# Instruction blocks of 256 in a kernel's planner, and the first group's joins written out chunk by chunk

## The chip, the cores and the metric

The kernel runs on one core of a Trainium2 chip. The metric is the device time of one execution in microseconds, the median of several runs. Engines: TensorE (PE, with its weight loads PEld), VectorE (DVE), ScalarE (ACT), GpSimd (POOL), and SyncE (SP), which issues the DMAs.

## The reference

A delta-rule attention runs over 768 tokens for 4 x 8 heads of width 48, and its output goes through a gated product with weights of 384 x 1536, 384 x 1536 and 1536 x 384.

```python
k_n = k / (np.linalg.norm(k, axis=-1, keepdims=True) + 1e-06)
state = np.zeros((B, H, D, D)); y = np.zeros_like(q)
for t in range(S):
    kt, vt, bt = k_n[:, :, t], v[:, :, t], beta[:, :, t, None]
    y[:, :, t] = einsum('bhd,bhde->bhe', q[:, :, t], state)
    v_old = einsum('bhde,bhd->bhe', state, kt)
    state = state + bt[..., None] * einsum('bhd,bhe->bhde', kt, vt - v_old)
x = y.transpose(0, 2, 1, 3).reshape(B * S, H * D)
out = ((x @ w_a) * (x @ w_b)) @ w_out
```

## The kernel before, in words

The 768 tokens are cut into 24 chunks of 32, the chunks into 6 groups of 4. All 32 heads are worked on together: 4 heads stand side by side on the 128 partitions, 8 times along the free axis, so that each step is a group of 32 small matmuls on a quarter of the array (each shows as 64 matmuls and 64 weight loads, since a float32 matmul is two).

For each group the program has three streams. `prep(g)` loads k, v and the transposed k and q, and makes the products of keys with keys and queries (matmuls `bank<-rawb`, or `late` for some chunks). `solve(g)` inverts the triangular matrices of the 4 chunks together on VectorE (lines 785 to 794, tiles `b` and `tmp`). In groups 0 and 1 (`HALVES`) only the two 16-wide diagonal halves are inverted so, and the rest is joined by matmuls, chunk by chunk: a product (`bank<-b,tt`, `wp`), a copy of it scaled by -1 on ScalarE (`wr`), a matmul that copies the halves into a bank (`bank<-b,mk`, `xp`), a product added to it (`bank<-wr,xn`), and a copy to `tt` on ScalarE. `steps(g)` carries the state through the chunks: for each chunk a copy `sh` of the state, products with it (`bank<-sh,rawb`), `f` on VectorE, the product with `tt` (`bank<-f,tt`; in chunk 0 `bank<-vnb,tt`), a copy `u`, the state's update (`S_ps<-u,knb`), the product `bank<-u,at`, and then y, its transpose, and the two float16 halves of x (`xb`). Two chunks make one block of 256 tokens of x.

The streams `w0` to `w11` decode one block of 128 columns of the three weights each and split it into two parts; for the first four (`LOWS`) the lower part is made with two matmuls (`bank<-wh,zi` and `bank<-wh,neg` and the like). `moe(s, fcs)` multiplies block s of x with weight blocks: two groups of nine matmuls (`bank<-xb,wh`), then the gate on ScalarE and VectorE (`a`, `g`, `ghl`), then in `moe_out` two groups of three matmuls (`bank<-wo,ghl`) that add up in banks kept over all the weight blocks of the call. `QUEUE` says which blocks of x meet which weight blocks first.

Nothing is issued in the order in which it is written. `Plan.add` collects the operations with an estimated duration; `Plan.link` finds what depends on what, from the order in which they were written and the memory that they touch; `Plan.order` then makes an order for each engine and all of them are issued so (line 449 issues every operation, line 440 the fillers). The order comes from `pack`, a list scheduler that goes through the time and gives each engine the ready operation of the lowest priority number: at first the place in the program less `URGENCY` and `BOOST` of its stream (group 0's streams and the product's other engines have the largest). A backward pass then gives new priorities, and it is done six times (`PASSES`); the order with the shortest planned total is kept. `pack` also gives out the PSUM banks: six in the pool, of which one is kept back until 60 us of planned time (`UNTIL`) for fillers, matmuls on a tile of ones that are issued wherever the planner sees TensorE idle after 1.5 us (`IDLE`, `SINCE`), so that its clock stays up.

For TensorE `pack` counts instructions as `words` (4 for a float32 matmul, 2 for another). Before, a store of 512 words (`STORE`) was filled again at 0.070 words per ns (`FETCH`), and an operation with more words than were in store was put off:

```python
words, seen = min(self.STORE, words + (t - seen) * self.FETCH), t
if words < ops[i].words:
    heapq.heappush(wait[e], (t + (ops[i].words - words) / self.FETCH + 1.0, i))
```

The order in which the streams are written down is at lines 1042 to 1051: all of `prep` and `solve` of group 0, weight blocks 0 and 1, all of group 0's `steps`, weight blocks 2 to 5; `merge` then takes product and group 1's streams in turns.

Of the kernel before, what the change touches and what calls it, by code (L numbers as in the profile page):

```python
# [28 lines left out]
GROUPS = [list(range(i, i + 4)) for i in range(0, NCH, 4)]  # L29
# [3 lines left out]
HALVES = [1, 1, 0, 0, 0, 0]  # L33
# [27 lines left out]
class Plan:  # L61
# [203 lines left out]
    def pack(self, pri, back=False):  # L265

        ops, n = self.ops, len(self.ops)
        nxt = self.pred if back else self.succ
        left = [len(x) for x in (self.succ if back else self.pred)]
        engs = sorted({o.eng for o in ops})  # L270
        wait = {e: [] for e in engs}
        can = {e: [] for e in engs}
        free = {e: 0.0 for e in engs}
        ready, at, stop, done, dma = [0.0] * n, [0.0] * n, [0.0] * n, [], 0.0
        until, use, warm = self.WINDOW, 0.0, back
        words, seen = self.STORE, 0.0
        kept = 0 if back else 1
        vacant, held, blocked = [(k, {}) for k in range(len(self.pool) - kept)], {}, []
        fill = {}
        for i, o in enumerate(ops):  # L280
            if not left[i]:
                heapq.heappush(wait[o.eng], (0.0, i))
        while len(done) < n:
            best = None
            for e in engs:
                if can[e]:
                    t = free[e]
                elif wait[e]:
                    t = max(free[e], wait[e][0][0])
                else:  # L290
                    continue
                if best is None or t < best[0]:
                    best = (t, e)
            if best is None:
                raise RuntimeError("no order found")
            t, e = best
            if kept and t >= self.UNTIL:
                kept = 0
                vacant.append((len(self.pool) - 1, {"PE": t}))
                for k in blocked:  # L300
                    heapq.heappush(wait[ops[k].eng], (t, k))
                blocked = []
            while wait[e] and wait[e][0][0] <= t:
                i = heapq.heappop(wait[e])[1]
                heapq.heappush(can[e], (pri[i], i))
            i = None
            while can[e] and i is None:
                i = heapq.heappop(can[e])[1]
                if ops[i].words and not back:
                    words, seen = min(self.STORE, words + (t - seen) * self.FETCH), t  # L310
                    if words < ops[i].words:
                        heapq.heappush(wait[e], (t + (ops[i].words - words) / self.FETCH + 1.0, i))
                        i = None
                        continue
                need = [] if back else [b for b in ops[i].banks if b not in held]
                if need:
                    at_ = sorted((self.clear(ends, i), k) for k, ends in vacant)
                    if len(at_) < len(need):
                        blocked.append(i)
                        i = None  # L320
                    elif at_[len(need) - 1][0] > t:
                        heapq.heappush(wait[e], (at_[len(need) - 1][0], i))
                        i = None
                    else:
                        for b, (_, k) in zip(need, at_):
                            held[b] = [k, self.users[b], {}]
                        vacant = [x for x in vacant if x[0] not in {k for _, k in at_[: len(need)]}]
            if i is None:
                continue
            o = ops[i]  # L330
            if not back and not o.banks and self.HOLD:

                soon = t + min(self.HOLD, 0.8 * o.dur)
                nxt_ = [r for r, k in wait[e] if t < r < soon and pri[k] < pri[i] - self.MARGIN]
                if nxt_:
                    heapq.heappush(can[e], (pri[i], i))
                    for x in can[e]:
                        heapq.heappush(wait[e], (min(nxt_), x[1]))
                    can[e] = []
                    continue  # L340
            at[i] = t
            words -= o.words
            if e == "PE" and not back:

                if kept:
                    f, took, many = max(free[e], self.SINCE), self.IDLE * (1 if warm else 2), 0
                    while f + took <= t:
                        while until <= f:
                            warm = use > 0.43 * self.WINDOW if warm else use > 0.75 * self.WINDOW
                            use, until = 0.0, until + self.WINDOW  # L350
                        took = self.IDLE * (1 if warm else 2)
                        use, f, many = use + took, f + took, many + 1
                    fill[i] = many
                    words = max(0.0, words - 4 * many)
                while until <= t:
                    warm = use > 0.43 * self.WINDOW if warm else use > 0.75 * self.WINDOW
                    use, until = 0.0, until + self.WINDOW
                took = o.dur if warm else o.cold
                full = took * o.use / o.dur
                part = min(1.0, (until - t) / took)  # L360
                use += full * part
                if part < 1.0:
                    warm = use > 0.43 * self.WINDOW if warm else use > 0.75 * self.WINDOW
                    use, until = full * (1 - part), until + self.WINDOW
            else:
                took = o.dur
            free[e] = end = stop[i] = t + took
            for b in () if back else o.banks:
                h = held[b]
                h[1] -= 1  # L370
                h[2][e] = max(h[2].get(e, 0.0), end)
                if not h[1]:
                    vacant.append((h[0], h[2]))
                    for k in blocked:
                        heapq.heappush(wait[ops[k].eng], (t, k))
                    blocked = []
            if e == "SP":
                if back:
                    end = t + o.dur + self.MOVE[0] + o.move + self.MOVE[1]
                else:  # L380
                    dma = max(dma, t + o.dur + self.MOVE[0]) + o.move
                    end = dma + self.MOVE[1]
            done.append(i)
            for k, late in nxt[i]:
                ready[k] = max(ready[k], end + late)
                left[k] -= 1
                if not left[k]:
                    heapq.heappush(wait[ops[k].eng], (ready[k], k))
        return at, stop, done, max(stop), ({b: h[0] for b, h in held.items()}, fill)

    MOVE = (900.0, 1100.0)
    FETCH = 0.070
    IDLE, SINCE, UNTIL = 440.0, 1500.0, 60e3
    STORE = 512.0
    SWITCH = 180.0
    HOLD = 300.0
    MARGIN = 5000.0
# [3 lines left out]
    def order(self):  # L401
# [3 lines left out]
        ops = self.ops  # L405
# [11 lines left out]
                self.pred[i].append((j, late))  # L417
        pri, best = [o.pri - boost(o) - 1e12 * (o.stream == 'load') for o in ops], None
        for _ in range(self.PASSES):
            at, stop, done, total, bind = self.pack(pri)  # L420
            if best is None or total < best[0]:
                best = (total, at, stop, done, bind)
            _, stop, _, total, _ = self.pack([-t for t in stop], True)
            pri = [k - 1e12 if o.stream == 'load' else total - t - boost(o) for k, (o, t) in enumerate(zip(ops, stop))]
# [28 lines left out]
def tile_kernel(ctx, tc, kqt, kn, vn, beta, w, masks, out):  # L453
    nc = tc.nc
    plan = Plan(nc)
# [311 lines left out]
    def solve(g):  # L767
# [35 lines left out]
        for ci, c in enumerate(chs):  # L803
            tts[c] = ttr()
            if HALVES[g]:
                wp = att()[:, 0:128].rearrange("p (q t) -> p q t", t=16)
                with plan.group():
                    for q, h4, _, _ in heads():
# [5 lines left out]
                            stop=True,  # L814
                            skip_group_check=True,
                        )
                wb_ = wr()
                A.activation(wb_, wp, AF.Copy, scale=-1.0)
                xp = att()[:, 0:256].rearrange("p (q t) -> p q t", t=32)
                T.matmul(xp, eye, xtv[:, ci], start=True, stop=True, skip_group_check=True)  # L820
                with plan.group():
                    for q, h4, _, _ in heads():
# [5 lines left out]
                            stop=True,  # L828
                            skip_group_check=True,
                        )  # L830
                A.copy(tts[c], xp)
            else:
                A.copy(tts[c], xtv[:, ci])
        yield

    def steps(g):

# [120 lines left out]
    ops = {}  # L958
# [38 lines left out]
    def run_all(gen):  # L997
        for _ in gen:
            pass
# [41 lines left out]
    V.tensor_scalar_mul(negr, eye, -1.0)  # L1041
    run_all(pr[0])
    next(ws[0])
    run_all(sv[0])
    run_all(ws[0])
    run_all(ws[1])
    run_all(st[0])
    queue.extend(QUEUE)
    run_all(ws[2])
    run_all(ws[3])  # L1050
# [91 lines left out]
```

## Time and profile before

| | |
|---|---|
| median of 3 runs | 665.3 us (662.72, 665.30, 665.31) |
| profiled execution | 666.49 us, its span 664.4 us |
| mean granted TensorE clock | 0.982 |
| TensorE busy | 633.4 us, 95% of the span |
| VectorE, ScalarE busy | 404.2 us (61%), 272.9 us (41%) |
| DMA of data | 41.08 MB |

In the rows of the profile an instruction's tiles stand as output<-inputs, by the names above, with its line (L449 or L440), its engine and how many are merged; "[1.64 <-issue]" is idle time of the engine before it and what ended it, and "issue" means that nothing that the profile shows was waited for. Clock is the share of full speed that TensorE was granted.

### The profile page before, as it was taken

To read this page: it belongs to the slowest core of one execution; us is meant where nothing else is said; L and a number is where in the kernel's file an instruction comes from. 1 tells how busy PE (TensorE), PEld (TensorE's weight loads), DVE (VectorE), ACT (ScalarE), POOL (GpSimd) and SP (SyncE) were. 2 spreads that over 40 slices of the span, in tenths; PEclk is the share of its full clock that TensorE was granted. 3 is DMA by queue.
4 is the path that set the end of the run, shared out by engine and by line. 5 is a ranking of instruction groups with operands and counts; after the bars stand their busy time and mean duration, and the time that the engine had idled before them with its cause. 6 is when DMAs were issued, how large, how long until landed. Compare 5 with 4: busy or idle time off the path is not lost.

```text
span 664.4 us, 26616 instructions
## 1 busy us (share of the span) xinstructions
PE 633.4 (95%) x12238; PEld 539.0 (81%) x12238; DVE 404.2 (61%) x1059; ACT 272.9 (41%) x599; POOL 21.5 (3%) x33
## 2 busy tenths in 40 slices
PE   9988899889999999899999899999999999999997
PEld 7756688678888888788888688877888887888886
DVE  6956699659757896447964438953537863322222
ACT  3345683355535634324543326253322253332322
POOL 0100000000001200000200002000000000000000
PEclk9969999979999999999999999999999999999999
DMA  6847200501482000033000410000000000000000
GB/s 234 304 167 256 75 3 2 200 20 34 166 297 75 2 25 3 4 139 111 2 25 5 161 65 26 1 26 4 4 2 26 1 26 5 2 25 1 25 1 24
DMA packets 19983, 42.77 MB, mean 64 GB/s; under 512 B 1184, under 2 KB 4512, under 8 KB 19872
## 3 DMA queue, kind: packets, MB, share of 16 engines
q1 hardware_dynamic: 19872, 41.08, 17.7%
q8 instruction: 95, 1.56, 1.0%
q14 instruction: 16, 0.13, 0.1%
HBM read 36.36 MB, written 4.72 MB: 62 GB/s over the span
## 4 chain that ended last, share of the span: by engine, by line
PE 80%; DVE 12%; issue 4%; ACT 3%; ACTq 0%
PE bank L449 74%; DVE b L449 4%; PE S_ps L449 3%; DVE tmp L449 3%; PE bank L440 3%; DVE ghl L449 1%; ACT tt L449 1%; DVE g L449 1%; ACT ghl L449 1%; ACT a L449 0%; DVE vnb L449 0%; ACT u L449 0%; DVE wh L449 0%; DVE sc L449 0%; ACT sqf L449 0%
## 5 line engine op out<-in xcount | busy, mean ns | idle before, releaser
L449 PEld LDWEIGHTS <-wh 128*128 128x128 f16 x2592 | 242.7, 99 | 48.0 <-issue 16.3
L449 PE MATMUL bank<-xb,wh 128*128 128x256 f16 x2160 | 259.5, 274 | 0.8 <-DVE wh L449 0.8
L449 PE MATMUL bank<-wo,ghl 128*128 128x384 f32 x864 | 189.9, 354 | 0.2 <-DVE ghl L449 0.2
L449 PEld LDWEIGHTS bank<-wo,ghl 128*128 128x128 f32 x864 | 144.2, 189 | 4.2 <-issue 0.9
L449 ACT COPY a<-bank 128x256 f32<-128x256 f32 x144 | 53.6, 372 | 199.9 <-PE bank L449 199.6
L449 DVE TENSOR_TENSOR g<-bank,a 128x256 f32<-128x256 f32 x144 | 60.8, 422 | 102.4 <-ACT a L449 101.2
L449 ACT CAST ghl<-g 128x256 fp32r<-128x256 f32 x144 | 58.1, 403 | 68.3 <-DVE g L449 67.8
L449 DVE TENSOR_TENSOR ghl<-g,ghl 128x256 fp32r<-128x256 f32 x144 | 61.3, 426 | 34.3 <-ACT ghl L449 32.4
L449 PE MATMUL bank<-late,wh 128*128 128x256 f16 x432 | 54.1, 278 | 0.0
L449 DVE TENSOR_TENSOR tmp<-b,b 128x31 f32<-128x31 f32 (+20 forms) x154 | 51.2, 332 | 2.9
L449 DVE TENSOR_TENSOR b<-b,tmp 128x31 f32<-128x31 f32 (+20 forms) x154 | 50.6, 328 | 2.7
L449 DVE SCALAR_TENSOR_TENSOR y<-bank,sc,y 128x384 f32<-128x384 f32 x23 | 14.2, 617 | 55.0 <-ACT y L449 55.0
L440 PE MATMUL bank<-ones 128*128 128x256 f32 x106 | 29.0, 430 | 1.0 <-DVE ones L449 1.0
L449 ACT COPY sh<-S_ps 112x768 f32<-112x768 f32 x23 | 18.4, 798 | 27.5 <-PE S_ps L449 27.3
L449 PEld LDWEIGHTS bank<-sh,rawb 48*64 48x64 f32 x1216 | 20.6, 134 | 11.1 <-issue 8.9
L449 PE MATMUL bank<-sh,rawb 48*64 48x48 f32 x1216 | 23.8, 221 | 5.3 <-issue 5.2
L449 PE MATMUL bank<-u,at 32*32 32x48 f32 x1536 | 23.4, 203 | 4.8 <-issue 4.8
L449 DVE TENSOR_TENSOR f<-vnb,bank 128x384 f32<-128x384 f32 x38 | 20.2, 545 | 10.5 <-PE bank L449 10.5
L449 PEld LDWEIGHTS bank<-u,at 32*32 32x32 f32 x1536 | 19.0, 105 | 8.7 <-issue 7.5
L440 PEld LDWEIGHTS bank<-ones 128*128 128x128 f32 x106 | 22.1, 215 | 4.5 <-DVE ones L449 1.0
L449 PEld LDWEIGHTS S_ps<-u,knb 32*48 32x48 f32 x1216 | 16.2, 123 | 10.6 <-ACT u L449 4.3
L449 PEld LDWEIGHTS bank<-f,tt 32*32 32x32 f32 x1472 | 17.6, 106 | 8.8 <-issue 4.1
(115 smaller groups left out, 550.6 us busy)
## 6 DMA issues: line engine op xcount, KB each, us to landing
late<-in_w SPq DMA_DIRECT2D x10, 1152.0 KB, 6.0
rawb<-in_kqt SPq DMA_DIRECT2D x10, 1024.0 KB, 7.7
out<-late SPq DMA_DIRECT2D x24, 192.0 KB, 1.9
knb<-in_kn SPq DMA_DIRECT2D x10, 384.0 KB, 4.2
vnb<-in_vn SPq DMA_DIRECT2D x10, 384.0 KB, 4.9
wh<-in_w SPq DMA_DIRECT2D x2, 1152.0 KB, 6.3
late<-in_kqt SPq DMA_DIRECT2D x2, 1024.0 KB, 5.7
late<-in_kn SPq DMA_DIRECT2D x2, 384.0 KB, 3.9
```

The source lines that it names most:

```text
L440: self.nc.tensor.matmul(self.pool[-1][:, 0:256], self.idle, self.idle.unsqueeze(1).broadcast_to([P, 2, P]), start=True, stop=True, skip_gr ...
L449: fn(*(self.place(a, lease) for a in args), **{k: self.place(a, lease) for k, a in kw.items()})
```

## The change

It has two parts. In `pack`, the store of words is replaced by blocks of 256 instructions: `pos` counts the instructions given out, `come` the times at which blocks are there. Two blocks are there at the start; when the first instruction of a block is given out, the next begins to load, and is there 3.5 us later, or 5.0 us if the planner's own DMA traffic is still under way. An operation that would reach a block before it is there is put off by the difference. The fillers count as well. A pass that finds no order now ends the search instead of the program.

In the program, group 0's joins are written out one chunk at a time, each followed by the three steps of its chunk; weight blocks 0 and 1 come behind all of them. In each join the matmul that copies the halves (`xp`) is given an extra dependency on the scaled copy (`wr`). In group 1 each join is a portion of its own in the turns with the product, four portions where there was one.

```diff
@@ -273,7 +273,7 @@
         free = {e: 0.0 for e in engs}
         ready, at, stop, done, dma = [0.0] * n, [0.0] * n, [0.0] * n, [], 0.0
         until, use, warm = self.WINDOW, 0.0, back
-        words, seen = self.STORE, 0.0
+        pos, come = 0, [0.0, 0.0]
         kept = 0 if back else 1
         vacant, held, blocked = [(k, {}) for k in range(len(self.pool) - kept)], {}, []
         fill = {}
@@ -292,7 +292,7 @@
                 if best is None or t < best[0]:
                     best = (t, e)
             if best is None:
-                raise RuntimeError("no order found")
+                return None
             t, e = best
             if kept and t >= self.UNTIL:
                 kept = 0
@@ -307,9 +307,9 @@
             while can[e] and i is None:
                 i = heapq.heappop(can[e])[1]
                 if ops[i].words and not back:
-                    words, seen = min(self.STORE, words + (t - seen) * self.FETCH), t
-                    if words < ops[i].words:
-                        heapq.heappush(wait[e], (t + (ops[i].words - words) / self.FETCH + 1.0, i))
+                    slip = self.fetch(t, ops[i].words, ops[i].dur if warm else ops[i].cold, pos, come, dma)[0]
+                    if slip > 1.0:
+                        heapq.heappush(wait[e], (t + slip, i))
                         i = None
                         continue
                 need = [] if back else [b for b in ops[i].banks if b not in held]
@@ -339,7 +339,8 @@
                     can[e] = []
                     continue
             at[i] = t
-            words -= o.words
+            if o.words and not back:
+                _, pos, come = self.fetch(t, o.words, o.dur if warm else o.cold, pos, come, dma)
             if e == "PE" and not back:
 
                 if kept:
@@ -351,7 +352,9 @@
                         took = self.IDLE * (1 if warm else 2)
                         use, f, many = use + took, f + took, many + 1
                     fill[i] = many
-                    words = max(0.0, words - 4 * many)
+                    if many:
+                        f0 = max(free[e], self.SINCE)
+                        _, pos, come = self.fetch(f0, 4 * many, f - f0, pos, come, dma)
                 while until <= t:
                     warm = use > 0.43 * self.WINDOW if warm else use > 0.75 * self.WINDOW
                     use, until = 0.0, until + self.WINDOW
@@ -389,9 +392,18 @@
         return at, stop, done, max(stop), ({b: h[0] for b, h in held.items()}, fill)
 
     MOVE = (900.0, 1100.0)
-    FETCH = 0.070
+    LOADED = (3500.0, 5000.0)
     IDLE, SINCE, UNTIL = 440.0, 1500.0, 60e3
-    STORE = 512.0
+
+    def fetch(self, t, n, took, pos, come, dma):
+        slip, come = 0.0, come[:]
+        for b in range(-(-pos // 256), -(-(pos + n) // 256)):
+            at = t + took * (b * 256 - pos) / n
+            slip = max(slip, come[b] - at)
+            if b + 1 == len(come):
+                at = max(at, come[b])
+                come.append(at + self.LOADED[at < dma])
+        return slip, pos + n, come
     SWITCH = 180.0
     HOLD = 300.0
     MARGIN = 5000.0
@@ -417,7 +429,10 @@
                 self.pred[i].append((j, late))
         pri, best = [o.pri - boost(o) - 1e12 * (o.stream == 'load') for o in ops], None
         for _ in range(self.PASSES):
-            at, stop, done, total, bind = self.pack(pri)
+            found = self.pack(pri)
+            if found is None:
+                break
+            at, stop, done, total, bind = found
             if best is None or total < best[0]:
                 best = (total, at, stop, done, bind)
             _, stop, _, total, _ = self.pack([-t for t in stop], True)
@@ -816,6 +831,7 @@
                         )
                 wb_ = wr()
                 A.activation(wb_, wp, AF.Copy, scale=-1.0)
+                plan.behind = {len(plan.ops) - 1}
                 xp = att()[:, 0:256].rearrange("p (q t) -> p q t", t=32)
                 T.matmul(xp, eye, xtv[:, ci], start=True, stop=True, skip_group_check=True)
                 with plan.group():
@@ -829,9 +845,11 @@
                             skip_group_check=True,
                         )
                 A.copy(tts[c], xp)
+                yield
             else:
                 A.copy(tts[c], xtv[:, ci])
-        yield
+        if not HALVES[g]:
+            yield
 
     def steps(g):
 
@@ -1041,10 +1059,14 @@
     V.tensor_scalar_mul(negr, eye, -1.0)
     run_all(pr[0])
     next(ws[0])
-    run_all(sv[0])
+    for _ in range(3):
+        next(sv[0])
+    for _ in GROUPS[0]:
+        next(sv[0], None)
+        for _ in range(3):
+            next(st[0], None)
     run_all(ws[0])
     run_all(ws[1])
-    run_all(st[0])
     queue.extend(QUEUE)
     run_all(ws[2])
     run_all(ws[3])
```

## The prediction

> **What bounds the kernel now.** I read the page first, then busy time by stretch, then what TensorE waited for, then the order in time around those waits and in the first 80 us. From the page: share of each engine, the granted clock in 40 slices, and the queue that brings instructions.
>
> ```profile
> PE 633.4 (95%) x12238; PEld 539.0 (81%) x12238; DVE 404.2 (61%) x1059; ACT 272.9 (41%) x599; POOL 21.5 (3%) x33
> ...
> PEclk9969999979999999999999999999999999999999
> ...
> q8 instruction: 95, 1.56, 1.0%
> ```
>
> TensorE is the bound (95%); no other engine passes 61%. The instruction queue q8 moved 95 packets and 1.56 MB, 16.4 KB each; TensorE ran 2 x 12,238 = 24,476 instructions, 258 for each packet. So its program comes in blocks of 256. The stretches (columns: stretch, length, busy time and count of PE, PEld, DVE, ACT, POOL, granted clock, DMA share, GB/s):
>
> ```profile
> 0.00:35.37 35.37, 32.37 (x607) 26.22 (x607) 28.22 (x80) 12.28 (x24) 3.75 (x13) 1.00 0.75 263
> 35.37:45.02 9.65, 8.83 (x256) 6.39 (x256) 4.21 (x15) 4.11 (x9) 0.00 (x0) 0.58 0.70 248
> ...
> 29.08:60.00 30.92, 27.25 (x815) 18.67 (x814) 19.80 (x35) 13.67 (x30) 2.12 (x2) 0.78 0.58 205
> 60.00:78.80 18.80, 15.07 (x539) 10.44 (x537) 11.56 (x25) 11.84 (x23) 0.00 (x0) 1.00 0.50 172
> 78.80:117.80 39.00, 38.24 (x755) 33.06 (x754) 35.74 (x112) 21.59 (x49) 0.00 (x0) 1.00 0.01 3
> 117.80:140.00 22.20, 17.91 (x624) 13.62 (x623) 11.04 (x22) 7.62 (x19) 0.95 (x1) 0.91 0.48 163
> 140.00:600.00 460.00, 446.29 (x8690) 386.25 (x8688) 287.11 (x755) 189.20 (x414) 16.84 (x19) 0.99 0.13 46
> ```
>
> TensorE idles 7.4 us in 29.08 to 78.8 (3.67 + 3.73), 0.8 to 117.8, 4.3 to 140, and 13.7 in the long stretch after it. What ended those waits (us, times, longest), in the whole span, in 29 to 140, and in 140 to 600:
>
> ```profile
> PE bank L449 <- issue: 18.4, 23, 2.4
> PE S_ps L449 <- issue: 1.9, 2, 1.3
> ...
> PE bank L449 <- issue: 9.4, 9, 2.4
> ...
> PE S_ps L449 <- issue: 0.7, 1, 0.7
> ...
> PE bank L449 <- issue: 9.0, 14, 1.8
> ...
> PE S_ps L449 <- issue: 1.3, 1, 1.3
> ```
>
> So 20.3 us in 25 waits went by with no other engine to blame. The order in time shows where they fall:
>
> ```profile
> 264.40 0.88 PE L449 MATMUL bank<-f,tt 32*32 32x48 f32 x64
> 265.22 1.10 PE L449 MATMUL bank<-rawb 48*32 48x64 f32 x64
> 266.25 0.48 PE L449 MATMUL S_ps<-u,knb 32*48 32x48 f32 x24
> 267.99 0.66 PE L449 MATMUL S_ps<-u,knb 32*48 32x48 f32 x40 [1.26 <-issue]
> 268.58 0.88 PE L449 MATMUL bank<-u,at 32*32 32x48 f32 x64
> 269.40 1.16 PE L449 MATMUL bank<-xb,wh 128*128 128x256 f16 x9
> 270.49 0.44 PE L449 MATMUL bank<-sh,late 48*64 48x48 f32 x14
> 271.57 0.96 PE L449 MATMUL bank<-sh,late 48*64 48x48 f32 x50 [0.64 <-issue]
> ...
> 380.94 0.32 PE L449 MATMUL bank<-sh,rawb 48*64 48x48 f32 x5 [1.81 <-issue]
> ```
>
> Each wait cuts a group of small matmuls in two, in the middle. From 267.99 to 271.57 there are 40 + 64 + 9 + 14 = 127 matmuls with their weight loads, 254 instructions: one block, in 3.58 us. The two stretches to 35.37 and 45.02 end at waits too, and 512 instructions, two blocks, lie between them. The waits are block fetches. Before 267.99, 152 small matmuls (304 instructions) passed in 2.3 us, faster than a block comes. Nine products (the row at 269.40) use 18 instructions in 1.16 us: they are what can fill the time.
>
> **The change, part by part.** (1) *Blocks in the planner.* Before, it let 0.070 instructions through per ns from a store of 512, which is one block per 3.66 us on average, but a burst of 512 goes through unseen. Now the next block starts to load as a block is entered and takes 3.5 us, or 5.0 while the planner believes DMA traffic is under way; a group that would reach a block's edge too early is put off and another operation goes ahead. Only the order changes: no instruction, no wait, no DMA is added by it. A quiet block took 3.58 us above, and the 5.0 is to be set against the loaded stretches: 1,629 instructions in 30.92 us (29.08 to 60, DMA share 0.58) are 4.9 us a block. Both constants fit.
>
> In 140 to 600 the issue waits are 9.0 + 1.3 = 10.3 of the 13.7 us idle, and in a stretch that is 97% busy there are products that can go first. So what is avoided is time won. The ends: nothing (edges guessed wrong), and all 10.3. One thing speaks for less than all: the first wait comes after 607 + 607 = 1,214 instructions, 190 past a multiple of 256, while the planner puts edges at multiples of 256 of its own count: a quarter of a block late. The filler it puts ahead of its edge falls ahead of the chip's edge in some cases and behind it in others, and where it is behind, it still lies in the next block. I take two thirds: **6.9 us**.
>
> (2) *Group 1's joins* (117.8 to 140): products have run out here, as these rows show, the first one the last first-half product before the stretch, the last the next:
>
> ```profile
> 118.54 1.16 PE L449 MATMUL bank<-xb,wh 128*128 128x256 f16 x9
> ...
> 135.98 0.86 PE L449 MATMUL bank<-f,tt 32*32 32x48 f32 x30 [2.36 <-issue]
> ...
> 138.60 2.08 PE L449 MATMUL bank<-xb,wh 128*128 128x256 f16 x9
> ```
>
> With little to fill, of the 4.3 us idle I take half, **2.1 us**. The 2.08 against 1.16 us is the clock at half after the wait: stretches at half clock are
>
> ```profile
> 36.94:50.59 13.65, 12.83 (x276) 8.72 (x275) 5.20 (x16) 6.68 (x14) 0.00 (x0) 0.50 0.50 175
> 135.92:142.75 6.83, 6.77 (x114) 5.65 (x114) 2.99 (x13) 3.25 (x6) 0.00 (x0) 0.50 0.01 2
> ```
>
> [...] With the waits halved I count **1 us**. The joins now come out in four portions between products in the program; their priority (boost 4e4) is above the product matmuls' either way, so that alone I cost at nothing; what hides it is that the joins' inputs all come at once.
>
> (3) *Group 0: each join, then that chunk's steps, and the copy matmul of a join held until its scaled copy is out.* The present order in the first 80 us:
>
> ```profile
> 32.16 0.37 ACT L449 COPY tt<-bank 128x256 f32<-128x256 f32 x1 [0.30 <-PE bank L449]
> ...
> 45.44 0.37 ACT L449 COPY tt<-bank 128x256 f32<-128x256 f32 x1 [1.11 <-PE bank L449]
> ...
> 51.43 0.48 ACT L449 CAST wo<-bank 128x384 fp32r<-128x384 f32 x1 [0.48 <-PE bank L449]
> ...
> 39.03 2.07 PE L440 MATMUL bank<-ones 128*128 128x256 f32 x4
> ...
> 42.46 1.20 PE L440 MATMUL bank<-ones 128*128 128x256 f32 x2
> ...
> 48.50 1.50 PE L449 MATMUL bank<-vnb,tt 32*32 32x48 f32 x64
> ...
> 58.80 1.54 PE L440 MATMUL bank<-ones 128*128 128x256 f32 x6
> ...
> 61.08 0.70 PE L440 MATMUL bank<-ones 128*128 128x256 f32 x2
> ...
> 73.40 0.91 PE L449 MATMUL bank<-wh,zi 128*128 128x384 f32 x2
> ...
> 78.80 2.12 PE L449 MATMUL bank<-xb,wh 128*128 128x256 f16 x18
> ```
>
> Chunk 0's join is done at 32.5, its first step (vnb,tt) runs at 48.50, after all four joins. Sixteen us of a serial chain are free to be moved. It ends in x for the first product, which starts at 78.80, while the first weight block was ready near 52 (wo at 51.43). Earlier products could fill the 7.4 us idle and replace the fillers (ones, 2.07 + 1.20 + 1.54 + 0.70 = 5.5 us): 12.9 us is the upper end. But this stretch holds 815 + 814 + 539 + 537 = 2,705 instructions, 10.6 blocks in 49.7 us, 4.7 us a block: fetch under DMA load sets its length, and products exist for two or three weight blocks only. The lower end is below nothing: the planner now sees waits in which it puts more fillers (they are issued whenever it sees TensorE idle before 60 us), and at 5.0 instead of 3.66 us for the 6.4 blocks up to 60 that is 8.5 us more. Fillers that take the place of a fetch wait cost nothing. Nearest to the idle rows, I take a third of 12.9: **4.3 us**. The DMAs and the weights' loads keep their order (loads stay first in every pass); the weights' own steps on ScalarE and VectorE now stand behind those of group 0 more often, hidden by the idle time there (13.67 of 30.92 us busy on ScalarE, 19.80 on VectorE, up to 60); were these engines full, each copy of a step (0.37 to 0.48 us in the rows above) would push the weights back by itself.
>
> **Sum.** 6.9 + 2.1 + 1 + 4.3 = 14.3 us. The profiled execution's time is 666.5 us (span 664.4), so 652.2; it stands 1.2 above the median of the runs, 665.3. Forecast for the median: 651.
>
> **The rivals.**
> *The planner's edges miss the chip's.* The quarter of a block, or a time scale that is off, leaves the waits where other groups now straddle the edge: (1) and (2) give nothing, only (3): 665.3 - 4.3 = 661. For it: the 1,214. Against it: the old rule had no edges at all.
> *All of it.* Both constants hold, products start before 60 us: 9 of the 10.3, the 4.3 with 2 of the clock, 8 of the 12.9 make 23: 642. For it: TensorE idles 0.8 us in 78.8 to 117.8 as soon as products are there. Against: fetch under load.
> *The start is taken back.* Products up to the sixth weight block run out at 118.54 now; begun earlier, they run out earlier, and the hole to 138.60 grows by what was won, unless group 1's solve moves too (VectorE is busy 35.74 of 39.00 us there). Then (3) is nothing: 655.
> *Banks: slower.* Up to 60 us five of six PSUM banks are to be had. Products begun before all six weight blocks are ready hold two for their sums; steps hold three; the correction terms of the weights (one bank each: 0.91 us for wh,zi, then a copy like the 0.48 of wo, near 2 us with the short matmul and the hand-overs) go one after another. Seven of them in line are 14 us, on the path because products wait for them: 665.3 - 10 + 14 = 669. It decides from 13 us of delay on. For it: the row at 73.40 shows the terms late already; against: the planner sees which banks are held.
> *Fetch is not the cause.* If the waits called issue come from something else, the order by blocks gains nothing in (1) and (2), and the time is the first rival's, 661. Against it: the block's 254 and 512 instructions between waits, and groups cut in the middle. [...]
>
> **How the numbers follow.** Forecast 0.45 (its own range 646 to 656); edges miss 0.20, with fetch not the cause in it at 0.03; all of it 0.14; the start taken back 0.11; banks 0.10. A measurement of this kernel tells from no change about 0.5%, 3.3 us: faster is under 662, slower over 668.6. Edges miss lies at that bound, six tenths of it faster. Faster: 0.45 + 0.14 + 0.11 + 0.12 = 0.82, less 0.05 for a forecast whose terms come out smaller, 0.77; same 0.08 + 0.05 = 0.13; slower 0.10, the banks. The range reaches from all of it to the edge of edges miss: 640 to 664.
>
> **What would show it.** Right: issue waits of TensorE fall from 20.3 to about 8 us; no half clock near 136; first vnb,tt before 40, first product (xb,wh) before 65; fillers after 29 us no more than 14; TensorE's busy time in the long stretch the same. Wrong: the same count of issue waits in groups cut in the middle (edges miss); many fillers between 29 and 60, a hole between products that ends later than 138.60, or wh,zi later than 73.40 (banks). The prediction is wrong most likely if the planner, given other costs, prefers quite another order.

## The result

The changed kernel takes 655.9 us (median of 4 runs, 654.23 to 656.65), the kernel before 664.0 us beside it: a ratio of 0.9877, 95% interval 0.9839 to 0.9914. Run once more on another chip it stood at 0.9892 (0.9849 to 0.9934). The forecast was 651, with 640 to 664 as its range.

The profile after, from the page (its lines L464 and L455 are what L449 and L440 were; in the other runs they stand a little further up or down):

```profile
PE 632.7 (97%) x12260; PEld 540.8 (83%) x12260; DVE 406.4 (62%) x1059; ACT 271.3 (42%) x599; POOL 19.8 (3%) x33
...
PEclk9969898999999999999999999999999999999999
...
q8 instruction: 96, 1.57, 1.0%
```

and by stretch (columns as in the prediction; the last row goes to 600 as the one before did):

```profile
29.08:60.00 30.92, 26.50 (x641) 19.76 (x641) 21.44 (x49) 12.14 (x27) 1.59 (x2) 0.83 0.55 197
60.00:78.60 18.60, 15.51 (x543) 11.34 (x542) 16.55 (x37) 14.55 (x29) 0.00 (x0) 0.91 0.51 192
78.60:117.80 39.20, 37.41 (x903) 32.40 (x903) 36.91 (x103) 23.25 (x51) 0.00 (x0) 0.96 0.27 93
117.80:140.00 22.20, 21.56 (x634) 16.89 (x636) 18.28 (x44) 11.15 (x26) 0.96 (x1) 1.00 0.17 57
140.00:600.00 460.00, 455.23 (x8825) 394.03 (x8812) 279.77 (x736) 184.46 (x413) 15.84 (x19) 1.00 0.13 43
```

From 140 to 600 TensorE idles 4.8 us instead of 13.7, from 117.8 to 140 0.6 instead of 4.3, and the granted clock is 1.00 in both (0.99 and 0.91 before). What it waited for after 140:

```profile
PE bank L464 <- issue: 2.8, 5, 1.6
PE bank L464 <- DVE g L464: 1.1, 4, 0.5
PE S_ps L464 <- ACT u L464: 0.6, 2, 0.3
```

The waits called issue, which the prediction takes for waits for instruction blocks, fell from 10.3 to 2.8 us there. The reader sees why in the order in time, at the place where the kernel before had three waits within 11 us:

```profile
261.00 2.14 PE L464 MATMUL bank<-xb,wh 128*128 128x256 f16 x18
263.07 0.88 PE L464 MATMUL bank<-u,at 32*32 32x48 f32 x64
263.88 0.79 PE L464 MATMUL bank<-wo,ghl 128*128 128x384 f32 x3
264.60 1.15 PE L464 MATMUL bank<-sh,late 48*64 48x48 f32 x64
265.68 0.79 PE L464 MATMUL bank<-wo,ghl 128*128 128x384 f32 x3
266.31 1.16 PE L464 MATMUL bank<-xb,wh 128*128 128x256 f16 x9
267.39 0.88 PE L464 MATMUL bank<-f,tt 32*32 32x48 f32 x64
```

Here no two groups of small matmuls stand back to back any more; a part of a product lies between each and the next.

The early part went the other way:

```profile
35.02 0.79 PE L464 MATMUL bank<-b,mk 128*128 128x256 f32 x1 [3.93 <-issue]
...
38.74 5.49 PE L455 MATMUL bank<-ones 128*128 128x256 f32 x12
...
45.08 0.88 PE L464 MATMUL bank<-vnb,tt 32*32 32x48 f32 x64
...
78.59 1.16 PE L464 MATMUL bank<-xb,wh 128*128 128x256 f16 x9
```

The first step of group 0 comes at 45.08 instead of 48.50 and the first product at 78.59 instead of 78.80: nothing was won. By 117.8 us less product is done. The same stretch by the tiles `xb` (the product's first half, `bank<-xb,wh`) and `ghl` (its second, `bank<-wo,ghl`) alone: the first two rows are the kernel before, the last two the changed one (second column TensorE's busy time and matmuls):

```profile
78.60:117.80 39.20, 22.22 (x189) 1.11 (x2) 0.90 (x2) 1.00 0.01 3
78.60:117.80 39.20, 10.69 (x48) 7.93 (x48) 3.73 (x9) 4.01 (x10) 1.00 0.01 3
...
78.60:117.80 39.20, 18.45 (x152) 1.12 (x2) 1.02 (x2) 0.96 0.27 93
78.60:117.80 39.20, 9.25 (x36) 6.68 (x36) 2.94 (x7) 2.81 (x7) 0.96 0.27 93
```

37 first-half matmuls fewer at 118 ns and 12 second-half ones at 223 ns (the first two rows' busy time by their counts) are 7.0 us of work left for later. (The 6 us in an expectation below is the same sum over all groups.) The two profiled spans differ by 664.4 - 653.3 = 11.1 us, so some 17 us were gained behind 118 us, 12.6 of them idle time (8.9 + 3.7), and 6 to 7 given up ahead of it. The remainder fits the clock: behind 118 us the kernel before runs at half clock (granted 0.50) twice, from 135.92 to 142.75 and in a stretch that the prediction does not list,

```profile
381.68:385.10 3.42, 3.42 (x17) 2.24 (x16) 0.64 (x2) 0.00 (x0) 0.00 (x0) 0.50 0.85 332
```

together 10.25 us; half of them, 5.1, is my estimate of the most that full clock would save. The changed kernel has no half clock there (1.00 from 117.8 to 600).

By 140 us the products stand even: 216 and 60 matmuls of the two halves after, 205 and 66 before. In a second profile of the changed kernel (span 657.5) 63 and 17 are missing at 117.8, 11.2 us, and 7 and 11 at 140, 3.3 us. So what the stretch from 117.8 to 140 gained is the debt of the early one, and what is kept was won behind 140 us. The experiments look for why.

### The profile page after: what moved, and what is told of

It is laid out like the page before. It is cut to its first block, busy times and chain, and to the rows that moved or that the text cites. A ratio compares the mean times of both kernels' runs of the same rounds, so it can differ in the third digit from the quotient of the medians.

```text
span 653.3 us, 26688 instructions
## 1 busy us (share of the span) xinstructions
PE 632.7 (97%) x12260; PEld 540.8 (83%) x12260; DVE 406.4 (62%) x1059; ACT 271.3 (42%) x599; POOL 19.8 (3%) x33
## 5 line engine op out<-in xcount | busy, mean ns | idle before, releaser
L464 PEld LDWEIGHTS <-wh 128*128 128x128 f16 x2592 | 242.2, 98 | 49.2 <-issue 19.9
L464 PE MATMUL bank<-xb,wh 128*128 128x256 f16 x2160 | 259.4, 273 | 2.3 <-issue 1.6
L464 PE MATMUL bank<-wo,ghl 128*128 128x384 f32 x864 | 189.7, 353 | 0.0
L464 PEld LDWEIGHTS bank<-wo,ghl 128*128 128x128 f32 x864 | 144.4, 190 | 4.0 <-issue 0.6
L464 ACT COPY a<-bank 128x256 f32<-128x256 f32 x144 | 53.5, 372 | 210.5 <-PE bank L464 210.4
L464 DVE TENSOR_TENSOR g<-bank,a 128x256 f32<-128x256 f32 x144 | 61.0, 423 | 117.5 <-ACT a L464 114.8
L464 DVE TENSOR_TENSOR ghl<-g,ghl 128x256 fp32r<-128x256 f32 x144 | 60.9, 423 | 37.4 <-ACT ghl L464 35.0
L464 ACT CAST ghl<-g 128x256 fp32r<-128x256 f32 x144 | 58.2, 404 | 56.6 <-DVE g L464 56.2
L464 PE MATMUL bank<-late,wh 128*128 128x256 f16 x432 | 52.5, 273 | 0.3 <-DVE g L464 0.3
L464 DVE TENSOR_TENSOR b<-b,tmp 128x31 f32<-128x31 f32 (+20 forms) x154 | 49.9, 324 | 3.6
L464 DVE TENSOR_TENSOR tmp<-b,b 128x31 f32<-128x31 f32 (+20 forms) x154 | 49.5, 322 | 3.3
L455 PE MATMUL bank<-ones 128*128 128x256 f32 x128 | 33.8, 421 | 1.1 <-DVE ones L464 1.1
L464 DVE SCALAR_TENSOR_TENSOR y<-bank,sc,y 128x384 f32<-128x384 f32 x23 | 14.2, 617 | 29.2 <-ACT y L464 28.7
L455 PEld LDWEIGHTS bank<-ones 128*128 128x128 f32 x128 | 26.4, 211 | 5.5 <-DVE ones L464 1.1
L464 PE MATMUL bank<-rawb 48*32 48x64 f32 x1280 | 22.9, 219 | 3.4 <-issue 1.9
L464 PEld LDWEIGHTS bank<-rawb 48*32 48x32 f32 x1280 | 19.2, 107 | 8.3 <-issue 4.2
L464 PEld LDWEIGHTS bank<-sh,rawb 48*64 48x64 f32 x1216 | 20.0, 134 | 4.6 <-issue 3.2
L464 ACT COPY sh<-S_ps 112x768 f32<-112x768 f32 x23 | 18.3, 797 | 13.0 <-PE S_ps L464 12.6
L464 PE MATMUL bank<-sh,rawb 48*64 48x48 f32 x1216 | 22.6, 220 | 0.7 <-issue 0.4
L464 PE MATMUL bank<-u,at 32*32 32x48 f32 x1536 | 22.1, 203 | 0.6 <-issue 0.6
L464 PEld LDWEIGHTS bank<-u,at 32*32 32x32 f32 x1536 | 18.5, 105 | 4.6 <-issue 4.0
L464 PEld LDWEIGHTS bank<-f,tt 32*32 32x32 f32 x1472 | 17.4, 105 | 5.9 <-issue 3.4
```

What stands on the lines that cost most here:

```text
L455: self.nc.tensor.matmul(self.pool[-1][:, 0:256], self.idle, self.idle.unsqueeze(1).broadcast_to([P, 2, P]), start=True, stop=True, skip_gr ...
L464: fn(*(self.place(a, lease) for a in args), **{k: self.place(a, lease) for k, a in kw.items()})
```

## The experiments

**Which part does what.** The joins alone, with the held copy matmul, under the old planner (a pass without an order ends the search there too; of the edit, group 0's program order is shown):

```diff
-    run_all(sv[0])
+    for _ in range(3):
+        next(sv[0])
+    for _ in GROUPS[0]:
+        next(sv[0], None)
+        for _ in range(3):
+            next(st[0], None)
     run_all(ws[0])
     run_all(ws[1])
-    run_all(st[0])
```

> The second part alone (group 0's joins chunk by chunk, the held copy matmul), with the old store of 512 words. Theory A, the gain is the block edges: TensorE's issue waits stay near 20 us in the whole span and near 10 us after 140 us, and the time stays within 4 us of the kernel before, 660 to 668. Theory B, the gain is the new order of the joins and steps: 652 to 658, with the first product (xb,wh) well before 78 us.

662.8 us, ratio 0.9953 (0.9923 to 0.9983). Its first step, first product and waits after 140 us:

```profile
35.08 1.50 PE L452 MATMUL bank<-vnb,tt 32*32 32x48 f32 x64 [2.21 <-issue]
...
66.65 2.13 PE L452 MATMUL bank<-xb,wh 128*128 128x256 f16 x9
...
PE bank L452 <- issue: 10.5, 18, 2.4
```

The issue waits stay (theory A), but the written-out joins do what they say: first step 13.4 us earlier than before, first product 12.2 us earlier. Little of it is kept: 2.7 us between the medians. By 140 us as many product matmuls are done as in the kernel before (202 and 66 against 205 and 66): the early start is taken back.

The blocks alone, that is the changed kernel with group 0's old program order:

```diff
-    for _ in range(3):
-        next(sv[0])
-    for _ in GROUPS[0]:
-        next(sv[0], None)
-        for _ in range(3):
-            next(st[0], None)
+    run_all(sv[0])
     run_all(ws[0])
     run_all(ws[1])
+    run_all(st[0])
```

> Blocks of 256 in the planner and the held copy matmul, but group 0's program order as before (all joins, two weight blocks, all steps). Theory A: the issue waits after 140 us fall to 2 to 4 us as in the changed kernel, and the time is that of the changed kernel or a few us less, 650 to 657, since the written-out joins gave nothing. Theory B: 661 or more.

670.9 us, ratio 1.0076 (1.0051 to 1.0102): slower than the kernel before. That is against theory A's time and within theory B's "661 or more", though neither named a loss. After 140 us the gain is there (issue waits 2.7 + 1.1 us). The loss lies ahead:

```profile
78.60:117.80 39.20, 10.41 (x72) 1.11 (x2) 1.01 (x2) 0.83 0.28 93
```

Only 72 first-half products in the stretch that had 189. So theory A is half of it: the blocks gain late and cost early, and the new joins take away about half of what they cost. (The old program with blocks and without the held copy matmul can't be had: the planner finds no order for it. So the held copy matmul has no run of its own.)

**What costs early: fillers, DMA, the place of an edge?** The changed kernel's very order without its late fillers:

```diff
-                for _ in range(self.fill.get(i, 0)):
+                for _ in range(self.fill.get(i, 0) if self.ops[i].at < 29e3 else 0):
```

> The changed kernel's very order, without the fillers that the planner put after 29 us of its time (34 records, 12.4 us of TensorE in the changed kernel's profile). Theory P, these fillers lie on the path: TensorE's early stretch gets 6 to 10 us shorter, time 645 to 650. Theory F, they only fill time in which TensorE would wait for its next block or for a hand-over: the fillers' time comes back as issue waits or other idle time between 29 and 80 us, time 653 to 658, perhaps 1 to 3 us more where the clock falls to half for longer.

659.5 us, 0.9907 (0.9879 to 0.9936), not faster. TensorE's busy time between 29.08 and 78.6 falls from 42.01 to 35.06 us, and the stretch gets no shorter: the first product stands at 81.71. Theory F: the fillers fill time that passes anyway. The granted clock of that stretch falls with them, from 0.86 to 0.74, so that a small cost of theirs could be hidden by it.

The same order with the loads of nine weight blocks left out (in `issue`, an operation in the set `skip` is passed over):

```diff
+        if what == "w" and c > 2:
+            plan.skip.add(len(plan.ops))
```

> The changed kernel's very order, but the loads of weight blocks 3 to 11 are left out (they are decoded again from what the slots hold, so the product is of other weights). Theory F2, instruction blocks come late because they queue with the weights' DMA: between 35 and 80 us a block takes 3.6 us instead of 5 to 6, issue waits there fall under 1 us and the time falls by 4 to 8 us, 648 to 652. Theory O, the early stretch is set by hand-overs between engines: time within 2 us of the changed kernel, 654 to 658, and the stretch to the first product is as long.

655.1 us, 0.9839 (0.9787 to 0.9892), as the changed kernel. First that one, then this one, from the first wait to 78.6:

```profile
35.02:78.60 43.58, 40.12 (x1054) 29.70 (x1054) 32.09 (x80) 26.14 (x53) 0.00 (x0) 0.85 0.50 181
...
35.30:78.60 43.30, 40.19 (x1056) 29.80 (x1057) 32.28 (x81) 26.44 (x53) 0.00 (x0) 0.84 0.14 46
```

The DMA share falls from 0.50 to 0.14 and the stretch takes as long for as many instructions. So the DMA load does not set its length. That points to the planned order and its hand-overs (theory O); the runs with another order, below, show that the order can shorten it.

Two more fillers ahead of the first join, eight instructions that move every edge:

```diff
+                more = 2 if self.fill.get(i, 0) and 20e3 < self.ops[i].at < 31e3 else 0
-                for _ in range(self.fill.get(i, 0)):
+                for _ in range(self.fill.get(i, 0) + more):
```

> The changed kernel's very order with two more filler matmuls (eight instructions) before group 0's first join, which starts 4 instructions ahead of a block's edge and meets a wait of 3.9 us one block later. Theory E, with the edge ahead of the join the next block is fetched while TensorE waits for the solve, and this wait goes: no issue wait over 1 us near 35 us, first join to first step 3 to 4 us shorter; time 0 to 4 us less than the changed kernel, 652 to 656. Theory F, the waits only move to the next block: the same sum of issue waits before 80 us and the time within 1 us.

656.0 us, 0.9807 (0.9765 to 0.9849); the changed kernel did not run beside it, and its own two intervals meet this one's end. The wait at that edge is gone (the row at 35.09 is the edge after it), and the first step is 6.5 us earlier, but a wait of 3.00 us stands two edges further on:

```profile
35.09 0.25 PE L465 MATMUL bank<-wr,xn 32*16 32x16 f32 x8 [0.19 <-issue]
...
38.62 0.88 PE L465 MATMUL bank<-vnb,tt 32*32 32x48 f32 x64
...
42.86 0.46 PE L465 MATMUL bank<-b,tt 32*32 32x16 f32 x26 [3.00 <-issue]
...
79.12 1.16 PE L465 MATMUL bank<-xb,wh 128*128 128x256 f16 x9
```

The first product does not follow: 79.12. From 29 to 80 us the issue waits sum to 4.5 us, against 4.6 in the changed kernel. So theory E has the wait and theory F the sum: the waits moved. That they hang on the place in the stream is shown here, since only positions were changed. That this one sets the early stretch is not so.

**Priorities or the rule?** One pass of the planner instead of six:

```diff
-    PASSES = 6
+    PASSES = 1
```

> The changed kernel with one pass of the planner instead of six, so that priorities are those of the order in which the program is written (the six passes had chosen priorities from a backward pass). Theory C, the early loss (the changed kernel has done 6 us less of TensorE's work by 118 us than the kernel before) comes from the backward priorities, which leave group 0's joins 2 and 3 to 72 us: joins and steps follow each other, first product before 72 us, time 646 to 652. Theory D, it comes from the block rule itself under DMA load, whatever the priorities: first product at 76 us or later, time 654 to 660.

673.0 us, 1.0064 (1.0036 to 1.0092), against theory C and worse than theory D's 654 to 660. The first product comes at 105.84, and before it TensorE goes from one small group to the next and waits in the middle of each second one:

```profile
81.09 0.84 PE L464 MATMUL bank<-u,at 32*32 32x48 f32 x27
83.14 1.01 PE L464 MATMUL bank<-u,at 32*32 32x48 f32 x37 [1.20 <-issue]
84.08 1.96 PE L464 MATMUL bank<-sh,rawb 48*64 48x48 f32 x64
85.97 2.16 PE L464 MATMUL bank<-rawb 48*32 48x64 f32 x64
88.06 1.50 PE L464 MATMUL bank<-f,tt 32*32 32x48 f32 x64
89.49 0.83 PE L464 MATMUL bank<-rawb 48*32 48x64 f32 x27
91.67 0.75 PE L464 MATMUL bank<-rawb 48*32 48x64 f32 x37 [1.35 <-issue]
...
105.84 8.28 PE L464 MATMUL bank<-xb,wh 128*128 128x256 f16 x54
```

The block of x that the products need is whole at about 73.6 here (the low half of the second chunk on VectorE, 73.00 and 0.56 us), so they were held back for 32 us, in which TensorE waited for blocks six times, 8.6 us in all. That led to the next theory.

The old store until a planned time, and blocks from there on (the lines that decide; the store's own bookkeeping comes back with them):

```diff
+                    words, seen = min(512.0, words + (t - seen) * 0.070), t
+                    if t < 80e3:
+                        slip = (ops[i].words - words) / 0.070 + 1.0 if words < ops[i].words else 0.0
```

> The changed program; the planner uses the old store of 512 up to 80 us of its time and blocks of 256 after that. Theory D, the blocks gain about 10 us after 140 us and cost about 6 us before 118 us: both come out, early stretch as in the kernel before or better, issue waits after 140 us under 5 us, time 645 to 651. If the two stretches can't be had apart, 654 to 658.

654.7 us, 0.9799 (0.976 to 0.9838): first step at 35.05, first product at 66.97, issue waits after 140 us 1.4 us. Both gains in one kernel, but above the 645 to 651 that were expected (the kernel before took 667.2 beside it).

> As the one before, with blocks from 100 us of planned time on: group 1's joins may fall under the old store again, with its two waits and the half clock near 135 us that the kernel before has (4.3 us idle). Theory D: 648 to 654, a few us more than with 80.

655.3 us, 0.981 (0.9771 to 0.9848): with 100 instead of 80 the waits after 140 us come back in part (5.5 us); the time is the same within the intervals, and a little above the expected 648 to 654.

**Room in the block.** A group of 32 float32 matmuls counts 128 instructions, so two of them fill a block of 256 exactly. The planner puts off only what would cross into a block before it is there. Two groups run to the edge; a product, last in priority, would now cross it and is put off too; when the block is there, the next group is ready and goes first. The test takes the kernel with one pass and changes one thing:

```diff
-                    slip = self.fetch(t, ops[i].words, ops[i].dur if warm else ops[i].cold, pos, come, dma)[0]
+                    more = 1 + 72 / 128 * (ops[i].words == 128)
+                    slip = self.fetch(t, int(ops[i].words * more), (ops[i].dur if warm else ops[i].cold) * more, pos, come, dma)[0]
```

> The kernel with one pass (673 us, first product at 105.8 us), with one thing changed: a group of 128 instructions is put off when it and 72 more would reach a block's edge too early, so that it leaves words of the block for products. Theory G, two groups of 128 fill a block of 256 exactly, the products, last in priority, come to the edge each time and are shut out until the groups are done: first product before 80 us, the 21 us lost by 118 us become 8 or less, time 653 to 661. Theory H, something else held the products (banks, weights): first product after 95 us, time 667 or more.

648.5 us, 0.9764 (0.9715 to 0.9813), where it was 1.0064: some 20 us for one line, more than theory G said. Products stand between the groups from 67.79 on:

```profile
67.79 1.23 PE L465 MATMUL bank<-xb,wh 128*128 128x256 f16 x9
68.95 0.72 PE L465 MATMUL bank<-wr,xn 32*16 32x16 f32 x64
69.60 1.16 PE L465 MATMUL bank<-xb,wh 128*128 128x256 f16 x9
70.70 1.20 PE L465 MATMUL bank<-f,tt 32*32 32x48 f32 x63
```

On the same chip the changed kernel, the store followed by blocks with room (54 in place of 72), and that one with the planner's count begun at 64:

> The changed kernel once more, on the chip of the next three, so that they can be compared with it: 0.983 to 0.991 of the kernel before.

657.7 us, 0.9892 (0.9849 to 0.9934).

> The version with the old store up to 80 us and blocks after that (0.980 of before), with room for 54 instructions left in a block by the groups of 128. Theory G: as that version or up to 5 us less, 646 to 654, ratio 0.970 to 0.980. If the room only spreads the groups, the same ratio within 0.003.

649.8 us, 0.9765 (0.9723 to 0.9807): in the expected range, and as fast as the kernel with room and one pass. Against the store and blocks without room (0.9799) that is 0.0034 less, with intervals that overlap, so this run does not tell what the room gives behind 80 us.

```diff
-        pos, come = 0, [0.0, 0.0]
+        pos, come = 64, [0.0, 0.0]
```

> The version before this one, with the planner's count begun at 64, where the chip's edges are. If the quarter of a block matters, issue waits after 140 us go from a few us to under 1 and the time falls by 1 to 3 us; if it doesn't, it stays within 1.5 us either way, since each block gets its filler all the same.

645.5 us, 0.9704 (0.9667 to 0.9741), the fastest: 20 us less than the kernel before and clear of the changed one. Waits after 140 us, first without and then with the edges aligned:

```profile
PE bank L471 <- issue: 5.7, 6, 1.8
...
PE bank L471 <- issue: 1.9, 2, 1.7
```

The waits fall by 3.8 us, which is nearly the 4.3 us between the two. The runs of the two, beside each other, lie apart (648.29 to 653.00 and 644.37 to 646.24). But the new count also gave another order, so that the alignment is the cause is likely and not shown.

## Why the prediction was right, and where it was wrong

**(1) Blocks after 140 us: right, in mechanism and size.** 6.9 us taken, 10.3 - 2.8 = 7.5 us of issue waits measured. No other wait took their place: all idle time there fell by 8.9 us. The kernels with blocks had 1.4 to 6.2 us of issue waits after 140 us, whatever their early part; the two without had 10.3 and 10.5.

**(2) Group 1's joins: right in sign, with another cause.** Idle time fell by 3.7 us (2.1 taken), and the half clock near 136 us is gone, as is the one near 382 that I had not counted. But the step "products have run out here" did not hold in the new order: 66 first-half products ran in this stretch instead of 18. They were there because they had been late before: with the products even by 140 us, or still 3.3 us short, this stretch paid a debt of the early one and won nothing of its own. No run shows the 1 us that the sum has for the clock. What the runs show is that groups of small matmuls take longer at a low clock: in the kernel with one pass (granted 0.53 from 84.00 to 90.30) the group `rawb` at 85.97 took 2.16 us against 1.10 at 265.22 in the kernel before (granted 1.00 from 264 to 272), and f,tt at 88.06 1.50 against 0.88 at 264.40. So the half clock can have cost well more than 1 us, up to 5.1 over both stretches. That the four portions in the program's turns cost nothing holds: written as one portion, TensorE's order comes out the same, instruction by instruction.

**(3) Group 0: wrong.** I took a gain of 4.3 us; it was a loss of some 6 to 7. The step that failed is the one that says the stretch is set by "fetch under DMA load" (at a DMA share of 0.14 instead of 0.50 TensorE did 1,056 matmuls in 43.30 us instead of 1,054 in 43.58) and that earlier products fill the idle time. The joins and steps did move when they stood alone (first product at 66.65), but the block rule took that back. The low half of x's second chunk, which makes the first block of x whole, in the joins alone and then in the changed kernel:

```profile
62.95 0.56 DVE L452 TENSOR_TENSOR xb<-yt,xb 128x384 f16<-128x384 f32 x1 [1.80 <-ACT xb L452]
...
71.21 0.55 DVE L464 TENSOR_TENSOR xb<-yt,xb 128x384 f16<-128x384 f32 x1
```

The two programs differ in the planner's rule alone, and of the 11.9 us by which the first product is later, 8.2 are x itself: under the rule the steps come later, not only the products. With the store up to 80 us x is whole at 64.63. That products were shut out of blocks filled to the edge is shown in the kernel with one pass; in the changed kernel at most the other 3.7 us can be that, and it is not shown for them. I had looked at the rule's times and not at what it lets through. Of the times, 3.5 us fits the 3.58 us of a quiet block; 5.0 is short in places: in the run with two more fillers 7.77 us lie between the waits at 35.09 and 42.86, which are one block apart. I bounded its harm by the fillers, 8.5 us; the fillers came (12 at 38.74 and more after), and the run without them was no faster.

**The sum** came out near by luck, because two errors met: behind 118 us some 17 us were gained where 10.0 had been taken (6.9 + 2.1 + 1; 7 of the 17 went into the products left over from ahead of 118 us), and ahead of it 6 to 7 were lost where 4.3 were to be won. 14.3 was forecast, 8.1 measured by the medians, 11.1 between the profiled spans.

**The signs.** Two came: issue waits of 9.6 us in the whole span (about 8 named), and no half clock near 136. Three did not: the first step at 45.08 (before 40 named), the first product at 78.59 (before 65), and 34 fillers after 29 us (at most 14). All three are of the early part. TensorE's busy time in the long stretch, named as the same, rose by 8.9 us, since its idle time was filled with products left over.

**The rivals.** *The planner's edges miss the chip's*: no; 7.5 of 10.3 us came without alignment, and the aligned kernel suggests that a few us are to be had by it. *All of it*: 642 was within reach, by 645.5 us, with a rule that leaves room. *The start taken back*: near in its time (655), but in the changed kernel there was no early gain to take back; in the kernel with the joins alone there was one, and it was taken back by 140 us. *Banks*: its time did not come, though two of its signs did, 32 fillers between 29 and 60 us where 12 had been and a last wh,zi at 77.77. No wait for a bank shows, and nine of the twelve copies of corrections were out by 67.73, 11 us ahead of the first product. The slower side existed: the block rule with the old program order, 670.9 us. I had no rival for it, because I priced the rule by its waits alone. *Fetch is not the cause*: fallen; eight more instructions, with the order unchanged, took away a wait of 3.93 us and put one of 3.00 us two edges further on. And the waits sit at one place of a block. Count the matmuls and weight loads before a wait: 1,214 at 35.37 in the kernel before, 958 at 35.02 in the changed one, 1,468 at 42.86 with two more fillers, which are 190, 190 and 188 past a multiple of 256. The same count over all 14 profiles, whatever their order, puts every one of the 186 issue waits of TensorE at 146 to 190, falling slowly and alike from 190 at the start.

## What to carry to other kernels

Count the instructions ahead of each issue wait of TensorE. Here all 186 stand at 146 to 190 past a multiple of 256; before one of 1.26 us, 304 instructions of small matmuls passed in 2.3 us, and the 254 behind it, up to the next wait, took 3.58 us. Where a trace shows the like, try long matmuls between the short ones: in the changed kernel, which does so, the waits after 140 us are 2.8 us instead of 10.3. A scheduler with such a limit must leave room in it for the work that is to fill the time; if the urgent groups fill a block exactly, the filler is shut out and TensorE stands still beside work that is ready (8.6 us in six waits with one pass; 673.0 us, and 648.5 with room). Look at a change of this kind by stretches, since a gain in the long part can hide a loss at the start (some 17 and 7 us here).

## What was not expected of the hardware

A wait of 3.93 us hung on where the first join stood to an edge. In the changed kernel 258 instructions lie between the join's first one and the wait, so that by the count the edge one block earlier stands 2 instructions behind the join's first one (the expectation above says 4). TensorE went on at 35.02 us, 5.8 us after the join began at 29.19. With eight more instructions in front, that edge lay ahead of the join, and there was no wait at the next one. Why the place of that edge decides, no trace or run shows.
